# A decode block on one core: whole key rows for three pairs, and diagonal sums moved behind the next pair's scores

## The chip, the core and the metric

The kernel runs on one NeuronCore of a Trainium2 chip. The metric is the device time of one execution in microseconds (us); smaller is better. Its engines appear in the profile as PE (TensorE: matrix products, with PEld for its weight loads), DVE (VectorE), ACT (ScalarE), POOL (GpSimd) and SP (SyncE, which here issues nearly all DMAs). Each engine runs its own list of instructions in order; semaphores order them against each other. Sixteen DMA engines move data between the device memory and the on-chip memory (SBUF); PE writes its results into PSUM, which has eight banks.

## What is computed

One token goes through an attention block with a cache of 16384 positions, and then through a small mixer with an MLP. What matters here is the attention:

```
q = (layernorm(x) @ wq)                       # 32 heads of 128
scores = einsum(q, k_cache) * 128 ** -0.5     # 8 key heads, each shared by 4 query heads
p = softmax(scores)
o = einsum(p, v_cache)
h = x + o.reshape(1, 1, 4096) @ wo
```

The two caches are [8, 16384, 128] in bf16, 33.5 MB each. With wq, wo and the weights of the MLP the core reads 79 MB in all and computes little with each byte.

## The kernel before, in words

The work of the attention goes in four *pairs* of key heads (`PAIRS = 4`, loop at the end of the kernel function, from `load_values(0)` on). The keys of a pair are 8 MB, laid out over 128 partitions with 64 KB each (`pair_rows`); the values likewise. There is one buffer for the keys of a pair, `kb_all`, seen as two halves `kb[0]` and `kb[1]` of 32 KB per partition, one buffer `vb` for the values, and one buffer `kt` for the transposed keys of half a pair.

For each pair j the order is:

1. `clear` (ACT) sets the two score banks to zero; DVE copies the pair's query into `qn` (L740).
2. For each half y: `transpose_keys` (DVE, L655) transposes blocks of the half from `kb[y]` into `kt`, eight *pieces* in one or more instructions; the list `cuts` says where an instruction begins, so `(0, 4)` are two instructions with four pieces each. `scores` (PE, L666) multiplies piece by piece, four matmuls each. A piece of `kt` may be overwritten when its matmuls have run. When the half is transposed, `load_keys` lets SP issue the same half of the next pair into `kb[y]` (L468).
3. `softmax`: DVE takes the maximum (L680), PE spreads it, DVE forms the bias (L687), ACT takes the exponential (L691), DVE transposes the probabilities into `pt` (L695).
4. `unread(16)`: PE runs 16 matmuls whose result nobody reads, in a small loop, between the spread of the maximum and the sums. The loop's length is fixed; it doesn't test whether `pt` is there.
5. `sums` (PE, and a reciprocal on DVE, L715), then `values` (PE, L706), 64 matmuls that wait for `pt` and, through an empty instruction on POOL, for the values' landing.
6. `gather`: DVE adds four blocks of the product up (L722, L725) into `od`, PE multiplies that by a mask (L728), DVE scales the diagonal blocks into `o_m` (L730). Then `load_values` lets SP issue the next pair's values, as soon as PE has read `vb`.

SP runs its list in order: the keys of pair j + 1 (two halves) and then the values of pair j + 1. DVE's list has `gather(j)` ahead of the transposes of pair j + 1. After the last pair come the product with `wo` (L775, loaded into `kb[0]`), a layer norm, and the MLP with `w3` and `w4` (L800, L828, L514, loaded into `kb[1]`), the last slice of `w4` as the last transfer.

PE's program is a real loop over the pairs (`_tensor`): it waits on one DVE semaphore, whose count must grow by the same amount in each pair. Therefore an instruction of DVE may carry a `worth` over one, and `SEEN` and `ROUND` say by how much POOL raises the values' semaphore. `P.part` names the section of the loop that an instruction belongs to.

The buffers that set the order around the change are `kb_all` (who has read it, before SP may refill it), `vb`, and `kt`.

Of the kernel before, what the change touches and what calls it, by code (L numbers as in the profile page):

```python
# [356 lines left out]
NCH = D // 128  # L357
# [4 lines left out]
WO = ((0, 20), (20, 32))  # L362
VP = 1

SEEN, ROUND = 47, 28
W3 = ((0, 4),)
W4 = ((0, 8), (8, 13), (13, 14))
PAIRS = HKV // 2
RPARTS = 6
QPAD = 4 * 7  # L370
KP = 8 * DH
# [9 lines left out]
def bass_sequential_preLN__gqa_block_cached__mixer_s_mlp__decode_kernel(  # L381
# [13 lines left out]
    with ExitStack() as ctx:  # L395
# [71 lines left out]
        def load(name, dst, src, key, by="SP", also=()):  # L467
            P.op(by, lambda e: e.dma_start(dst, src), w=[key, *also], dma=name)  # L468
# [24 lines left out]
        def dve(fn, r=(), w=(), bank=(), own=None):  # L493
            return P.op("DVE", fn, r, w, bank, own=own)
# [7 lines left out]
        def pe(fn, r=(), w=(), bank=(), also=(), times=None, many=1):  # L502

            return P.op("PE", fn, r, w, bank, also=also, times=times, many=many)

        def unread(times):
            field = qb[:, :, :, :].rearrange("p a j q -> p (a j q)")
            P.op("PE", lambda e: e.matmul(O_ps[1][:, :], field[:, 0:128], field[:, 0:512], start=True, stop=True),  # L508
                 r=["qb"], bank=[("O", 1)], times=times)
# [77 lines left out]
        load("wq0", wq_sb[:, 0:WQ], wq_in[:, 0:WQ], "wq0")  # L587
        load("wq1", wq_sb[:, WQ:NCH * HQ * DH], wq_in[:, WQ:NCH * HQ * DH], ("v", 0), also=[("v", x) for x in range(1, VP)])
        load_keys(0, 0)
        load_keys(0, 1)  # L590

        dve(lambda e: e.memset(mean4[:, :], -1.0 / (32 * D)), w=["mean4"])
        pool(lambda e: e.memset(ident_f[:, :], 0.0), w=["ident_f"])
# [54 lines left out]
                qcol[lo:hi, :, :, 0].rearrange("p n (j h) -> p n j h", h=REP)), r=["qcol"], w=["qb"])  # L648


        def transpose_keys(y, cuts):
            for t, n in zip(cuts, [b - a for a, b in zip(cuts, [*cuts[1:], 8])]):
                view = lambda x, t=t, n=n: x[:, :].bitcast(I32).rearrange("p (x l w) -> p x (l w)", x=2, l=64)[
                    :, :, t * 512:(t + n) * 512]
                P.op("DVE", lambda e, view=view: e.transpose(view(kt), view(kb[y])),  # L655
                     r=[("r", y, i) for i in range(RPARTS)], w=[("kt", t + i) for i in range(n)], worth=n)

        def key_piece(at, n):
            part = kt[:, :].rearrange("p (x f) -> p x f", x=2)[:, :, bass.ds(at, KP)]
# [18 lines left out]
        def softmax(j):  # L678

            dve(lambda e: e.tensor_reduce(mx[:, :], s_all, AX.X, ALU.max), r=[("s", 0), ("s", 1)], w=["mx"], **both)  # L680
# [6 lines left out]
            dve(lambda e: e.scalar_tensor_tensor(nmh[:, :], nm[:, :, :].rearrange("p g h -> p (g h)"),  # L687
                                                 32 * D * SCALE, zd[:, :].rearrange("p (n d) -> p n d", d=4)[:, :, 0],
                                                 ALU.mult, ALU.mult, accum_out=bias[:, :]),
                r=["nm", "zd"], w=["nmh", "bias"])  # L690
            act(lambda e: e.activation(p_sb[:, :], s_all, ACTF.Exp, bias=bias[:, 0:1], scale=float(SCALE),  # L691
                                       accum_out=acc[:, :]),
                r=[("s", 0), ("s", 1), "bias"], w=["p", "acc"], **both)
            for g in range(2):
                dve(lambda e, g=g: e.transpose(pt[64 * g:64 * g + 64, :, :, g, :], p_sb[64 * g:64 * g + 64, :]),  # L695
                    r=["p"], w=["pt"])
# [14 lines left out]
        def sums(j):  # L711

            pe(lambda e: e.matmul(n_ps[0:32, 32:33], zd[:, :], acc[:, :], start=True, stop=True),  # L713
               r=["acc", "zd", "pt"], w=["n"], bank=["mn"])
            dve(lambda e: e.reciprocal(den[:, :], n_ps[0:32, 32:33]), r=["n"], w=["den"], bank=["mn"])  # L715
        def gather(j):

            O, key = O_ps[0], ("O", 0)
            for c in range(4):
                block = O[:, c * 128:(c + 1) * 128]  # L720
                if c == 0:
                    dve(lambda e, block=block: e.tensor_scalar(od[:, :], block, rowc[:, 0:1], None, ALU.mult),  # L722
                        r=[key, "rowc"], w=["od"], bank=[key])
                else:
                    dve(lambda e, block=block, c=c: e.scalar_tensor_tensor(  # L725
                        od[:, :], block, rowc[:, c:c + 1], od[:, :], ALU.mult, ALU.add),
                        r=[key, "rowc", "od"], w=["od"], bank=[key])
            pe(lambda e: e.matmul(A_ps[0:32, 0:128], zo[:, :], od[:, :], start=True, stop=True),  # L728
               r=["od", "zo"], w=["A"], bank=["A"])
            dve(lambda e: e.scalar_tensor_tensor(  # L730
                o_m[32 * j:32 * j + 32, :, :], A_ps[0:32, 0:128].rearrange("p (d r) -> p d r", d=4), den[:, 0:1],
                maskdd[0:32, :].unsqueeze(2).to_broadcast([32, 4, 32]), ALU.mult, ALU.mult),
                r=["A", "den", "maskdd"], w=["o_m"], bank=["A"])
# [24 lines left out]
        for n, (lo, hi) in enumerate(WO):  # L758
# [114 lines left out]
```

## Time and profile before

| | us |
|---|---|
| median of 3 runs | 189.6 (189.52 to 189.7) |
| the profiled execution | 189.84 |
| its span, first to last instruction | 188.5 |
| DVE busy, of that: transposes of keys (L655, 25 instructions) | 116.6, 70.6 |
| PE busy, of that: scores (L666, 256 matmuls) | 131.4, 70.1 |
| mean time of one value matmul / one score matmul | 0.379 / 0.416 |

Times of single instructions come from the profiled execution, counted from the start of its span. In a row of the timeline the first number is the start, the second the duration; then come the engine, the line of the kernel, the operation, the output and its inputs, the shapes, the number of instructions merged into the row, and in brackets how long the engine had been idle and for whom. In a row of the groups, busy time and the mean duration in ns follow the bar, then idle time and what ended it. A row of the DMA view gives the size and the time from issue to landing; "SPq" rows of the timeline give the issue. A row of the stretches gives the stretch, its length, the busy time of PE, PEld, DVE, ACT and POOL with the number of instructions, the granted TensorE clock (1.00 is full), the busy share of the DMA engines and their GB/s.

### The profile page before, as it was taken

Reading aid. Unit: us, or ns where it says so; the run is one execution under the profiler, and the core shown is the slowest. Engines: PE = TensorE matmul, PEld = TensorE weight load, DVE = VectorE, ACT = ScalarE, POOL = GpSimd, SP = SyncE. Lnnn points to the kernel's source line nnn. Section 1 sums busy time; section 2 is a strip of 40 time slices with the busy share of each in tenths; the row PEclk is TensorE's granted clock in tenths of the full one; section 3 lists DMA queues with packets and bytes.
Section 4 is the critical chain, followed back from the end, with each engine's and each line's share of the span. In section 5 each row is a group of like instructions: output and inputs, shape, how many; then the busy total and the mean of one; then the engine's idle time right before and its main releaser. Section 6 shows DMA issues by size and latency. Waiting matters only on the chain.

```text
span 188.5 us, 2406 instructions
## 1 busy us (share of the span) xinstructions
PE 131.4 (70%) x767; PEld 51.1 (27%) x767; DVE 116.6 (62%) x139; ACT 13.7 (7%) x21; POOL 4.6 (2%) x8
## 2 busy tenths in 40 slices
PE   0109902978879419888794198887947999696783
PEld 0103401333324203333242033332422333133321
DVE  5740599699152597891525978915259997543165
ACT  3000100000040000000400000004000000320012
POOL 8100000000000000000000000000000000000000
PEclk9999985599999966999999669999996999999789
DMA  6999999999799999988999999997999999969994
GB/s 227 468 417 445 445 445 445 445 445 445 334 445 445 445 556 417 431 348 382 424 445 445 445 445 445 445 445 341 438 445 445 556 445 431 431 297 404 423 414 162
DMA packets 2895, 79.19 MB, mean 420 GB/s; under 512 B 334, under 2 KB 462, under 8 KB 718
## 3 DMA queue, kind: packets, MB, share of 16 engines
q1 hardware_dynamic: 2886, 79.17, 97.7%
q8 instruction: 1, 0.02, 0.0%
q10 hardware_dynamic: 8, 0.00, 0.0%
HBM read 79.17 MB, written 0.00 MB: 420 GB/s over the span
## 4 chain that ended last, share of the span: by engine, by line
PE 51%; DVE 35%; DMA 6%; issue 6%; ACT 0%; SPq 0%; DVEq 0%; ACTq 0%
DVE kt L655 25%; PE banks L666 20%; PE banks L508 12%; PE banks L706 8%; DMA vb<-in_A_wq_dram 6%; PE banks L632 5%; DVE mx L680 3%; PE banks L775 2%; DVE od L725 2%; PE banks L683 1%; PE banks L728 1%; DVE od L722 1%; DVE qcol L639 1%; DVE mxd L681 1%; PE banks L828 1%
## 5 line engine op out<-in xcount | busy, mean ns | idle before, releaser
L666 PE MATMUL banks<-kt,qn 128*128 x256 | 70.1, 416 | 25.6 <-DVE kt L655 25.4
L655 DVE STREAM_TRANSPOSE kt<-kb 128x4096 int32<-128x4096 int32 (+2 forms) x25 | 70.6, 2878 | 5.2 <-PE banks L666 5.2
L666 PEld LDWEIGHTS banks<-kt,qn 128*128 x256 | 26.2, 102 | 68.9 <-issue 53.5
L508 PE MATMUL banks<-qb 128*128 128x512 bf16 x70 | 25.6, 389 | 0.6
L706 PE MATMUL banks<-vb,pt 128*32 128x512 bf16 x256 | 14.7, 379 | 0.0
L632 PE MATMUL banks<-vb,xn 128*128 x32 | 10.0, 489 | 6.7 <-DVE xn L623 6.7
L691 ACT ACTIVATE p_sb<-banks,bias 128x1024 bf16<-128x1024 f32 x4 | 4.5, 1114 | 132.7 <-DVE nmh L687 132.7
L680 DVE TENSOR_REDUCE mx<-banks 128x1 f32<-128x1024 f32 x4 | 4.9, 1225 | 14.6 <-PE banks L666 14.6
L695 DVE STREAM_TRANSPOSE pt<-p_sb 64x1024 bf16<-64x1024 bf16 x8 | 9.9, 1239 | 5.4 <-ACT p_sb L691 5.3
L508 PEld LDWEIGHTS banks<-qb 128*128 128x128 bf16 x70 | 6.7, 97 | 18.8 <-issue 18.5
L706 PEld LDWEIGHTS banks<-vb,pt 128*32 128x32 bf16 x256 | 9.3, 97 | 3.5
L639 DVE STREAM_TRANSPOSE qcol<-banks 64x1024 f32<-64x1024 f32 x4 | 4.8, 1227 | 8.2 <-PE banks L632 8.2
L722 DVE TENSOR_SCALAR od<-banks,rowc 128x128 f32<-128x128 f32 x4 | 1.4, 350 | 13.4 <-PE banks L706 13.4
L632 PEld LDWEIGHTS banks<-vb,xn 128*128 128x128 bf16 x32 | 3.8, 120 | 12.5 <-issue 10.6
L683 PE MATMUL banks<-mxd,mean 128*128 128x128 f32 x8 | 2.0, 326 | 6.6 <-DVE mxd L681 6.6
L728 PE MATMUL banks<-od,zo 128*32 128x128 f32 x8 | 1.6, 285 | 6.5 <-DVE od L725 6.5
L675 ACT ACTIVATE banks<-mean 128x1024 f32<-128x1024 f32 x4 | 4.1, 1027 | 20.1 <-DVE qcol L639 20.0
L775 PE MATMUL banks<-kb,o_b 128*32 128x512 bf16 x44 | 4.6, 550 | 1.1 <-DVE o_b L771 1.1
L715 DVE RECIPROCAL den<-banks 32x1 f32<-32x1 f32 x4 | 0.6, 155 | 6.9 <-PE banks L713 6.9
L725 DVE SCALAR_TENSOR_TENSOR od<-banks,rowc,od 128x128 f32<-128x128 f32 x12 | 4.2, 351 | 0.4
L601 PE MATMUL banks<-x,quarter 4*128 4x128 bf16 x1 | 0.3, 281 | 5.4 <-DVE quarter L599 5.4
L599 DVE CAST quarter<-ident_f 4x128 bf16<-4x128 f32 x1 | 3.2, 3229 | 1.0 <-DMA x<-in_A_x_dram 1.0
(71 smaller groups left out, 39.9 us busy)
## 6 DMA issues: line engine op xcount, KB each, us to landing
kb<-in_A_k_cache_dram SPq DMA_DIRECT2D x8, 4096.0 KB, 25.5
vb<-in_A_wq_dram SPq DMA_DIRECT2D x1, 3584.0 KB, 11.7
kb<-in_A_wo_dram SPq DMA_DIRECT2D x1, 2560.0 KB, 24.1
kb<-in_B_w_dram SPq DMA_DIRECT2D x1, 1792.0 KB, 23.1
kb<-in_A_wo_dram SPq DMA_DIRECT2D x1, 1536.0 KB, 27.4
kb<-in_B_w_dram SPq DMA_DIRECT2D x1, 1024.0 KB, 25.2
kb<-in_B_w_dram SPq DMA_DIRECT2D x1, 640.0 KB, 26.3
vb<-in_A_wq_dram SPq DMA_DIRECT2D x1, 512.0 KB, 3.7
```

Of the source, the lines that this page charges most:

```text
L508: P.op("PE", lambda e: e.matmul(O_ps[1][:, :], field[:, 0:128], field[:, 0:512], start=True, stop=True), r=["qb"], bank=[("O", 1)], times= ...
L632: pe(lambda e, k=k: e.matmul(row[:, bass.ds(P.b + P.b0, 512)], copies(xn[:, k:k + 1], 128), wq_k[:, k, bass.ds(P.c + P.c0, REP * DH)], sta ...
L639: dve(lambda e, g=g, b=b, half=half: e.transpose(qcol[64 * g:64 * g + 64, 2 * b:2 * b + 2, :, :].rearrange("p e m u -> p (e m u)"), half.r ...
L655: P.op("DVE", lambda e, view=view: e.transpose(view(kt), view(kb[y])), r=[("r", y, i) for i in range(RPARTS)], w=[("kt", t + i) for i in r ...
L666: pe(lambda e, n=n: e.matmul(row[:, bass.ds(P.y, 512)], qn[:, n, bass.ds(P.q, 128)], key_piece(P.k, n), start=False, stop=(n == 3), skip_g ...
L675: act(lambda e: e.activation(s_all, copies(mean4[:, 0:1], 1024), ACTF.Identity, scale=0.0), r=["mean4", "p"], w=[("s", 0), ("s", 1)], **both)
L680: dve(lambda e: e.tensor_reduce(mx[:, :], s_all, AX.X, ALU.max), r=[("s", 0), ("s", 1)], w=["mx"], **both)
L691: act(lambda e: e.activation(p_sb[:, :], s_all, ACTF.Exp, bias=bias[:, 0:1], scale=float(SCALE), accum_out=acc[:, :]), r=[("s", 0), ("s", ...
L695: dve(lambda e, g=g: e.transpose(pt[64 * g:64 * g + 64, :, :, g, :], p_sb[64 * g:64 * g + 64, :]), r=["p"], w=["pt"])
L706: pe(lambda e, l=l, ct=ct, ch=ch: e.matmul(O_ps[0][32 * ct:32 * ct + 32, :], pt[:, l, ch, :, :].rearrange("p g u -> p (g u)"), tiles[:, l ...
L725: dve(lambda e, block=block, c=c: e.scalar_tensor_tensor(od[:, :], block, rowc[:, c:c + 1], od[:, :], ALU.mult, ALU.add), r=[key, "rowc", ...
L775: pe(lambda e, r_=r_, q=q: e.matmul(O_ps[0][32 * q:32 * q + 32, :], copies(o_b[:, r_:r_ + 1], 32), wo_sb[:, r_ * D:(r_ + 1) * D], start=(r ...
```

## The change

The keys of pairs 0 to 2 come as one transfer with whole rows of 64 KB, issued once the second half of the pair before has been read; pair 3 still comes in halves. ACT copies the last two of the eight pieces of the second half into a new buffer `aside`, and DVE transposes these two from there, so its last read of `kb_all` is one instruction earlier. The cuts change: the second half of pairs 0 to 2 takes three instructions with 4, 2 and 2 pieces, pair 3 takes (2, 2, 4) and (4, 2, 1, 1) instead of (1, 1, 2, 2, 2) and eight single ones. `gather` of pair j moves behind the transposes of pair j + 1 on DVE (`rows`, its matmul, behind the scores on PE; `spread`, its last step, behind the bias). For pair 0, where nothing is to be gathered, DVE zeroes `od`. The reciprocal goes along with `gather`. `unread` makes 12 rounds instead of 16. `SEEN` follows the new counts.

```diff
-SEEN, ROUND = 47, 28
+SEEN, ROUND = 53, 28
+WHOLE, ASIDE = PAIRS - 1, 2
+LAST = ((0, 2, 4), (0, 4, 6, 7))
...
+        aside = sb("aside", [128, 2, ASIDE * KP], BF16)
...
         def load_keys(j, y):
             n = 128 * DH
+            if j < WHOLE:
+                load("k0", kb_all[:, :], pair_rows(A_k_cache, j), ("r", 0, 0),
+                     also=[("r", 0, i) for i in range(1, RPARTS)] + [("r", 1, i) for i in range(RPARTS)])
+                return
             load(f"k{y}", kb[y][:, :], pair_rows(A_k_cache, j)[:, y * n:(y + 1) * n], ("r", y, 0),
...
         load_keys(0, 0)
-        load_keys(0, 1)
...
+        def put_aside():
+            act(lambda e: e.copy(aside[:, :, :], pieces(kb[1], 8 - ASIDE, ASIDE)),
+                r=[("r", 1, i) for i in range(RPARTS)], w=["aside"])
+
+        def transpose_keys(y, cuts, from_aside=False):
             for t, n in zip(cuts, [b - a for a, b in zip(cuts, [*cuts[1:], 8])]):
+                last = from_aside and t == 8 - ASIDE
+                of = aside[:, :, :] if last else pieces(kb[y], t, n)
+                P.op("DVE", lambda e, of=of, t=t, n=n: e.transpose(pieces(kt, t, n).bitcast(I32), of.bitcast(I32)),
+                     r=["aside"] if last else [("r", y, i) for i in range(RPARTS)],
+                     w=[("kt", t + i) for i in range(n)], worth=n)
...
+            spread(j - 1)
...
+        def gather(j):
+            P.part("late", j)
+            if j < 0:
+                P.op("DVE", lambda e: e.memset(od[:, :], 0.0), w=["od"], worth=1 + NCH)
+                return
             dve(lambda e: e.reciprocal(den[:, :], n_ps[0:32, 32:33]), r=["n"], w=["den"], bank=["mn"])
...
+        def rows(j):
             pe(lambda e: e.matmul(A_ps[0:32, 0:128], zo[:, :], od[:, :], start=True, stop=True),
                r=["od", "zo"], w=["A"], bank=["A"])
...
+            if j < WHOLE:
+                put_aside()
             for y in range(2):
                 P.part("half", j, y)
-                transpose_keys(y, (0, 4) if j < PAIRS - 1 else range(8) if y else (0, 1, 2, 4, 6))
+                if j < WHOLE:
+                    transpose_keys(y, (0, 4, 8 - ASIDE) if y else (0, 4), from_aside=y == 1)
+                else:
+                    transpose_keys(y, LAST[y])
                 scores(j, y)
-                if j < PAIRS - 1:
+                if j < PAIRS - 1 and (y or j + 1 >= WHOLE):
                     load_keys(j + 1, y)
+            gather(j - 1)
             P.part("middle", j)
+            rows(j - 1)
             softmax(j)
-            unread(16)
+            unread(12)
             sums(j)
             values(j)
-            P.part("rest", j)
-            gather(j)
             if j < PAIRS - 1:
                 load_values(j + 1)
+        P.part()
+        gather(PAIRS - 1)
+        P.part()
+        rows(PAIRS - 1)
+        spread(PAIRS - 1)
```

More of the change, by code (lines that the diff above doesn't have):

```diff
@@ L648, in bass_sequential_preLN__gqa_block_cached__mixer_s_mlp__decode_kernel, with pieces @@
                 qcol[lo:hi, :, :, 0].rearrange("p n (j h) -> p n j h", h=REP)), r=["qcol"], w=["qb"])
-        def transpose_keys(y, cuts):
-            for t, n in zip(cuts, [b - a for a, b in zip(cuts, [*cuts[1:], 8])]):
[L653 to L656, printed above, removed]
+        def pieces(x, t, n):
+            return x[:, :].rearrange("p (x l) -> p x l", x=2)[:, :, t * KP:(t + n) * KP]
+        def put_aside():
+            act(lambda e: e.copy(aside[:, :, :], pieces(kb[1], 8 - ASIDE, ASIDE)),
+                r=[("r", 1, i) for i in range(RPARTS)], w=["aside"])
+        def transpose_keys(y, cuts, from_aside=False):
+            for t, n in zip(cuts, [b - a for a, b in zip(cuts, [*cuts[1:], 8])]):
+                last = from_aside and t == 8 - ASIDE
[3 more added lines that the diff above has]
+                     w=[("kt", t + i) for i in range(n)], worth=n)
         def key_piece(at, n):
@@ L686, in softmax @@
                                           AX.X, ALU.min), r=["m"], w=["nm"], bank=["mn"])
-            dve(lambda e: e.scalar_tensor_tensor(nmh[:, :], nm[:, :, :].rearrange("p g h -> p (g h)"),
+            P.op("DVE", lambda e: e.scalar_tensor_tensor(nmh[:, :], nm[:, :, :].rearrange("p g h -> p (g h)"),
                                                  32 * D * SCALE, zd[:, :].rearrange("p (n d) -> p n d", d=4)[:, :, 0],
                                                  ALU.mult, ALU.mult, accum_out=bias[:, :]),
-                r=["nm", "zd"], w=["nmh", "bias"])
+                r=["nm", "zd"], w=["nmh", "bias"], worth=1 + (j == 0))
+            spread(j - 1)
             act(lambda e: e.activation(p_sb[:, :], s_all, ACTF.Exp, bias=bias[:, 0:1], scale=float(SCALE),
@@ L714, in sums @@
                r=["acc", "zd", "pt"], w=["n"], bank=["mn"])
-            dve(lambda e: e.reciprocal(den[:, :], n_ps[0:32, 32:33]), r=["n"], w=["den"], bank=["mn"])
         def gather(j):
             O, key = O_ps[0], ("O", 0)
+            P.part("late", j)
+            if j < 0:
+                P.op("DVE", lambda e: e.memset(od[:, :], 0.0), w=["od"], worth=1 + NCH)
+                return
+            dve(lambda e: e.reciprocal(den[:, :], n_ps[0:32, 32:33]), r=["n"], w=["den"], bank=["mn"])
             for c in range(4):
@@ L727, in gather, with spread @@
                         r=[key, "rowc", "od"], w=["od"], bank=[key])
+        def rows(j):
             pe(lambda e: e.matmul(A_ps[0:32, 0:128], zo[:, :], od[:, :], start=True, stop=True),
                r=["od", "zo"], w=["A"], bank=["A"])
+        def spread(j):
+            if j < 0:
+                P.count["DVE"] += 1
+                return
             dve(lambda e: e.scalar_tensor_tensor(
```

## The prediction

> **What bounds the kernel now.** I read the page first: busy shares, the DMA row of the slices, the queues, the chain of the end.
>
> ```profile
> span 188.5 us, 2406 instructions
> PE 131.4 (70%) x767; PEld 51.1 (27%) x767; DVE 116.6 (62%) x139; ACT 13.7 (7%) x21; POOL 4.6 (2%) x8
> DMA  6999999999799999988999999997999999969994
> q1 hardware_dynamic: 2886, 79.17, 97.7%
> PE 51%; DVE 35%; DMA 6%; issue 6%; ACT 0%; SPq 0%; DVEq 0%; ACTq 0%
> ```
>
> The chain names PE and DVE for 86% of the span, and DVE's transposes and PE's scores do alternate in it. But the queue row says that the 16 DMA engines were busy 97.7% of the span. A chain shows only who came last at each step; a resource that never rests can hide behind it. So next I asked the stretches view for everything between the first bytes and the last ones, and the DMA view and SP's timeline, transfer by transfer (issue time in the one, us from issue to landing in the other).
>
> ```profile
> 2.00:186.00 184.00, 130.41 (x715) 50.36 (x718) 115.74 (x137) 12.76 (x20) 3.32 (x2) 0.92 1.00 430
> ```
> ```profile
> 2.12 0.43 SPq L468 DMA_DIRECT2D kb<-in_A_k_cache_dram  x1
> 23.90 0.33 SPq L468 DMA_DIRECT2D vb<-in_A_v_cache_dram  x1
> 46.97 0.33 SPq L468 DMA_DIRECT2D kb<-in_A_k_cache_dram  x1
> 122.47 0.33 SPq L468 DMA_DIRECT2D kb<-in_A_k_cache_dram  x1
> 138.42 0.33 SPq L468 DMA_DIRECT2D vb<-in_A_v_cache_dram  x1
> 160.34 0.43 SPq L468 DMA_DIRECT2D kb<-in_B_w_dram  x1
> ```
> ```profile
> kb<-in_A_k_cache_dram SPq DMA_DIRECT2D x1, 4096.0 KB, 30.2
> vb<-in_A_v_cache_dram SPq DMA_DIRECT2D x1, 27.8
> kb<-in_A_k_cache_dram SPq DMA_DIRECT2D x1, 4096.0 KB, 24.1
> kb<-in_A_k_cache_dram SPq DMA_DIRECT2D x1, 4096.0 KB, 26.2
> vb<-in_A_v_cache_dram SPq DMA_DIRECT2D x1, 29.6
> kb<-in_B_w_dram SPq DMA_DIRECT2D x1, 128.0 KB, 26.1
> ```
>
> From 2 to 186 us the DMA share is 1.00 at 430 GB/s: the stream has no hole. Adding the rows pairwise gives landings: keys 0 (second half) 32.3 us, values 0 51.7, keys 1 71.1, keys 3 148.7, values 3 168.0, the last slice of w4 186.4. Eight MB of keys in rows of 32 KB took 71.1 − 51.7 = 19.4 us, of values in rows of 64 KB 168.0 − 148.7 = 19.3: a difference of the size of the view's 0.1 us. From keys 1 to keys 3, two pairs, it was 77.6 us, so 19.4 for each 8 MB; that puts values 1 at 90.5, keys 2 at 109.9. Now the end, against that last landing:
>
> ```profile
> 185.98 0.99 PE L828 MATMUL banks<-kb,hcol 128*32 128x128 bf16 x52 [1.54 <-DVE hcol L816]
> 186.80 0.23 PE L514 MATMUL banks<-kb,hcol 128*32 128x128 bf16 x4
> ```
>
> The four matmuls that use the last slice start at 186.80, only 0.4 us after it landed. So the kernel has **two chains that end together**: the stream, and PE/DVE 0.4 us behind it. Whatever the edit gives PE and DVE, about 0.4 us of it can reach the end, plus what the stream itself gains.
>
> **The change, part by part.** *Keys of pairs 0 to 2 as one transfer.* The same bytes; three issues fewer on SP (each about 0.3 us there, beside a full queue: nothing). The gain by longer rows lies between 0 and 0.1 us per pair, by the 19.4 and the 19.3; I take 0.2 us for three, and keep 0 to 0.3. The price is lateness: the first half of keys can no longer be used while the second is on its way. Both halves now land at 32.3, 71.0, 109.7 us. At 71.0 the transposes start 5.5 us later than now, as they began at 65.53:
>
> ```profile
> 27.39 8.77 DVE L655 STREAM_TRANSPOSE kt<-kb 128x4096 int32<-128x4096 int32 x2
> 38.12 8.77 DVE L655 STREAM_TRANSPOSE kt<-kb 128x4096 int32<-128x4096 int32 x2 [1.97 <-PE banks L666]
> 65.53 8.75 DVE L655 STREAM_TRANSPOSE kt<-kb 128x4096 int32<-128x4096 int32 x2
> 75.97 8.77 DVE L655 STREAM_TRANSPOSE kt<-kb 128x4096 int32<-128x4096 int32 x2 [1.69 <-PE banks L666]
> 89.05 1.23 DVE L680 TENSOR_REDUCE mx<-banks 128x1 f32<-128x1024 f32 x1 [4.31 <-PE banks L666]
> 160.61 1.22 DVE L680 TENSOR_REDUCE mx<-banks 128x1 f32<-128x1024 f32 x1 [1.67 <-PE banks L666]
> 164.58 2.49 DVE L695 STREAM_TRANSPOSE pt<-p_sb 64x1024 bf16<-64x1024 bf16 x2 [1.33 <-ACT p_sb L691]
> ```
> ```profile
> L655 DVE STREAM_TRANSPOSE kt<-kb 128x4096 int32<-128x4096 int32 x12 | 52.6, 4420 | 5.2 <-PE banks L666 5.2
> L655 DVE STREAM_TRANSPOSE kt<-kb 128x2048 int32<-128x2048 int32 x3 | 6.7, 2271 | 0.0
> ```
>
> *Does the stream stay full?* With one buffer for keys and one for values, keys j+1 must be issued while values j are still arriving. They are issued when the third transpose of the second half has read the buffer (the last two pieces are read from `aside`). Counted from the first transpose: third big one 75.97 − 65.53 = 10.4 us, plus half a pair of them 4.4, plus a two-piece one 2.3: 17.1 us (pair 0: 10.7 + 4.4 + 2.3 = 17.4). Values j land 19.4 us after keys j. So the issue comes 2.0 us (pair 0) and 2.3 us (pairs 1, 2) ahead of the end of the queue. Now values 0 are issued at 23.90, 8.4 us before keys 0 have landed; then only these 2 us are left. The nearest price of an issue into an empty queue is the first transfer of the kernel:
>
> ```profile
> 0.73 0.40 SPq L468 DMA_DIRECT2D vb<-in_A_wq_dram  x1
> vb<-in_A_wq_dram SPq DMA_DIRECT2D x1, 512.0 KB, 3.7
> ```
> ```profile
> DMA packets 18, 0.04 MB, mean 105 GB/s; under 512 B 8, under 2 KB 8, under 8 KB 18
> ```
>
> The second fence is the DMA view of 1.6 to 2.0 us: its packets of 4 KB are the first rows of this transfer, so data flow at most 1.3 us after the issue at 0.73. From above: it landed after 3.7 us, of which 0.5 MB at 430 GB/s are 1.2, so at most 2.5 us are not data. I take 1.3, the direct sighting; then the stream stays full with 0.7 us to spare. Cost 0, with up to 2.5 kept for the range. The Trainium skill, "DMA: Bandwidth & Descriptors", section "Anatomy of one DMA", speaks against the change here: it puts the fixed cost of one DMA at about 2.0 us. It adds that most of this is the receipt of the write, behind the data; if all 2.0 stood ahead of the data, pair 0 would be at its limit, an estimate of 0.0 to 0.1 us lost. No run shows yet which part stands ahead.
>
> *The copy to `aside`* is 4096 elements on ACT; by the clear of 1024 elements it is an estimate of 4 × 1.03 = 4.1 us.
>
> ```profile
> L675 ACT ACTIVATE banks<-mean x4: 1027/1027/1027, 22.8 to 130.7; 128x1024 f32<-128x1024 f32 x4
> ```
>
> ACT has nothing else between clear and exponential, and the reader comes 15 us later: nothing. ACT's wait on the keys holds up only that exponential. Without that cover the fourth transpose would wait, and PE with it.
>
> *Diagonal sums behind the next scores.* These rows are its price:
>
> ```profile
> L725 DVE SCALAR_TENSOR_TENSOR od<-banks,rowc,od 128x128 f32<-128x128 f32 x12 | 4.2, 351 | 0.4
> L728 PE MATMUL banks<-od,zo 128*32 128x128 f32 x8 | 1.6, 285 | 6.5 <-DVE od L725 6.5
> L730 DVE SCALAR_TENSOR_TENSOR o_m<-banks,den,maskdd 32x128 f32<-32x128 f32 x4 | 1.4, 341 | 2.0 <-PE banks L728 2.0
> ```
>
> Four operations on O (4 × 0.35 = 1.4 us) and a reciprocal leave the stretch between values and transposes; they now fill DVE's wait for the scores (4.31 us in the row at 89.05), `rows` (two passes, 0.4 us on PE) lies beside the 1.2 us maximum, `spread` (0.3) inside the 1.33 us wait for the exponential: nothing while these waits last, some 2.2 us per pair if they went. In pairs 0 to 2 the stretch won buys no time: DVE, ready at 32.4 + 23.8 + 6.5 = 62.7 us (steps below), stands before keys that land at 71.0. PE's `unread` loop, 12 in place of 16, ends 1.5 us sooner; there too it waits for values or keys. POOL's one signal per pair stays. Only pair 3, whose keys come in halves, and the tail turn PE/DVE work into time.
>
> *Pair 3, step by step.* Keys 2 land at 109.7, transposes start 109.8. To the maximum it took 89.05 − 65.53 = 23.5 us (0.3 more in pair 0, whose third transpose came 10.7 us in); the split last transpose spares PE 0.2: 133.1. From maximum to the end of the probabilities' transposes it took 164.58 + 2.49 − 160.61 = 6.5: 139.6. The copy of the query, 0.2, then the first half's transposes (8.8): 139.8 to 148.6. Now they begin at 141.0:
>
> ```profile
> 140.99 17.96 DVE L655 STREAM_TRANSPOSE kt<-kb 128x1024 int32<-128x1024 int32 x13
> 152.42 8.16 PE L666 MATMUL banks<-kt,qn 128*128 x32 [0.24 <-DVE kt L655]
> 162.54 6.00 PE L508 MATMUL banks<-qb 128*128 128x512 bf16 x16
> 168.53 0.19 PE L713 MATMUL banks<-acc,zd 128*32 128x1 f32 x1
> ```
>
> The second half lands at 148.7 − 0.2 = 148.5, so it follows at 148.6: a first transpose of four pieces 4.4, the hand-over 0.2, then 8.16 of scores: 161.4, **0.8 us later** than the 160.61 of now, because a big first piece makes PE wait. But behind it PE no longer idles through 16 `unread`: now 162.54 + 6.00 = 168.53, though DVE was done at 164.58 + 2.49 = 167.07. New: 161.4 + 6.5 = 167.9, the sums and then the values at 168.0 to 168.1, 0.4 to 0.5 us earlier. Values 3 land at 168.0 − 0.2 = 167.8, just before.
>
> *The sum.* The compute chain reaches the tail 0.45 us earlier. The last slice lands at 186.2; the last matmuls can start no earlier, so at most 186.80 − 186.25 = 0.55 can be won. Forecast 0.4 to 0.45 us: 189.84 → 189.4 against the profiled run's own time (189.84, span 188.5 and 1.3 around it). The median of the three runs, 189.6, lies 0.2 below that run; there I expect **189.2 us**. A difference under 0.2% (0.38 us) is about what a measurement here cannot tell from none; the forecast stands right at that edge.
>
> A rule that would give more: the same page, "Where 436 GB/s comes from", gives a port ceiling of 435.2 GB/s. The 430 of the row agree to 1%; if long rows lifted the 25 MB of keys to the ceiling, an estimate of 0.7 us would be spared and the sum would be 188.7. The values' 64 KB rows, at 19.4 us, show no such thing.
>
> **The rivals.** *(a) The end does not move.* The unprofiled runs may have their PE/DVE chain already at the last landing, the longer rows may be worth nothing, or the 0.8 us later scores may cost more than the shorter `unread` spares: 0 to 0.25 us won, 189.35 to 189.6. For it: every gain above is smaller than a us. *(b) Slower: a hole in the stream.* Keys j+1 issued too late, behind the third transpose. It decides when the lead needed exceeds 2.0 us; at the 2.5 from above it loses 0.5 + 0.2 + 0.2 = 0.9 us, and a PE at half clock one us longer (its share is 0.92 on the mean) as much again in a pair. 189.6 − 0.4 + 0.9 to 1.9 = 190.1 to 191.1; 190.2 by the first. Against it: the sighting at 1.3. *(c) Pair 3 late:* if the transposes there wait for pair 2, its scores slip by a us more, 0.6 us behind now: 190.1. *(d) It does what it says:* transposes at once after each softmax. A period is (140.99 − 65.53) / 2 = 37.7 us, so 65.53 + 37.7 − (89.05 + 6.5) = 7.7 us per pair, 3 × 7.7 = 23: 167. The stream forbids it: 79.17 MB at 430 GB/s are 184.1 us.
>
> **How the numbers follow.** Forecast (0.25 to 0.55 won) 0.54, of which 0.41 lie beyond 0.2% and 0.13 within; (a) 0.22, within; (b) 0.16 slower; (c) 0.06 slower; (d) and the faster rate 0.02. Faster 0.43, same 0.35, slower 0.22. The range runs from 189.0 (all 0.55 won) to 190.3, which takes in (a), (c) and the lower half of (b); about 0.12 is left out. The forecast's own range is 189.0 to 189.4.
>
> **What would show it.** DMA share 1.00 through 51.7, 90.5 and 129 us, and values 3 landing 0.2 us earlier: stream right; a dip there with a later landing: (b). DVE idle before the first key transposes of pairs 1 and 2 with a DMA as releaser, 8 us each. Maximum of pair 3 near 161.4, values near 168.1. The last four matmuls under 0.2 us behind the last landing. I am wrong if the last landing moves by more than 0.4 us either way.

## The result, and the profile after

The changed kernel takes **190.47 us** (median of 10 runs, 190.15 to 191.38) against 189.62 us before (10 runs, 189.5 to 189.84). The ratio is 1.005, 95% interval 1.0036 to 1.0063: half a per cent slower. The ten runs scatter over 1.2 us where the ten of before scatter over 0.3; beside the experiments the kernel before scattered over 0.8 to 1.0 us in 20 to 23 runs, so the scatter alone says little. The forecast was 189.2, in a range that ended at 190.3. All ratios, here and below, compare fast runs: a run more than 1.5% above the fastest of its kernel is left out (four in `e7`, one in `e5`).

The page of the changed kernel: span, the DMA row and the GB/s of the 40 slices, the chain of the end by engine and by line, and the group of the key transposes.

```profile
span 189.4 us, 2348 instructions
DMA  6999999999959999999999999997999999899994
GB/s 226 466 415 443 443 443 443 443 443 443 429 249 443 443 429 443 443 443 443 443 443 443 443 443 443 443 443 332 443 429 443 512 401 401 374 428 419 434 414 177
DMA 54%; DVE 23%; PE 18%; issue 3%; SPq 1%; ACT 1%; DVEq 0%; ACTq 0%
DMA kb<-in_A_k_cache_dram 39%; DVE kt L668 20%; PE banks L680 18%; DMA kb<-in_B_w_dram 14%; DVE pt L710 1%; SPq L471 1%; DVE mx L694 1%; ACT p_sb L706 1%; PE banks L697 0%; PE banks L865 0%; DVE qn L767 0%; DVE nm L699 0%; DVE mxd L695 0%; DVE fin L872 0%; DVE nmh L701 0%
L668 DVE STREAM_TRANSPOSE kt<-kb 128x4096 int32<-128x4096 int32 (+2 forms) x19 | 63.8, 3407 | 29.4 <-DMA kb<-in_A_k_cache_dram 23.2
```

The chain that named PE and DVE now names the DMA: DVE waits 23.2 us for keys that land whole. The DMA row has one new digit, the 5 in the twelfth slice (52 to 57 us), 249 GB/s there. Such a digit is a hint and no more: the view counts a packet where it starts, and packets of 64 KB start in rounds 2.42 us apart, so that the row of before has a 7 in its eleventh slice although nothing is lost there. The last slice of the GB/s row and the first belong to the two ends, as before. The whole stream:

```profile
2.00:187.00 185.00, 123.41 (x729) 49.73 (x729) 115.74 (x135) 23.57 (x23) 3.32 (x2) 0.87 1.00 428
```

SP's timeline (issues) and the DMA view (us to landing) show which transfer lost time: values 0, keys 1, values 1, keys 2, last slice of `w4`.

```profile
23.53 0.33 SPq L471 DMA_DIRECT2D vb<-in_A_v_cache_dram  x1
50.31 0.33 SPq L471 DMA_DIRECT2D kb<-in_A_k_cache_dram  x1
66.88 0.33 SPq L471 DMA_DIRECT2D vb<-in_A_v_cache_dram  x1
89.03 0.33 SPq L471 DMA_DIRECT2D kb<-in_A_k_cache_dram  x1
160.75 0.45 SPq L471 DMA_DIRECT2D kb<-in_B_w_dram  x1
```
```profile
vb<-in_A_v_cache_dram SPq DMA_DIRECT2D x1, 28.1
kb<-in_A_k_cache_dram SPq DMA_DIRECT2D x1, 21.8
vb<-in_A_v_cache_dram SPq DMA_DIRECT2D x1, 24.5
kb<-in_A_k_cache_dram SPq DMA_DIRECT2D x1, 21.9
kb<-in_B_w_dram SPq DMA_DIRECT2D x1, 128.0 KB, 26.8
```

Values 0 land at 51.6, keys 1 at 72.1: 20.5 us for 8 MB that took 19.4 before. Values 1 land at 91.4 (19.3 later), keys 2 at 111.0 (19.55). The last slice lands at 187.6 instead of 186.5. So 1.1 us were lost at **keys 1**, issued 1.3 us before the landing of values 0, and they stay lost to the end. The span grew by less, some 0.8 us, because the tail behind the last landing is shorter, 189.4 − 187.6 = 1.8 us instead of 2.1.

The packet records of the trace (start and duration of every DMA packet) show where the 1.1 us went. The 16 engines end their last data of values 0 between 50.80 and 51.17 us. Their first packets of keys 1 start between 51.28 and 52.26, so an engine stood idle for 0.55 us on average. And these first packets are slow. The DMA view of 51.25 to 52.30 us has just the 16 of them, the view of 54.15 to 55.20 the 16 behind them:

```profile
q1 hardware_dynamic: 16, 1.05, 288.1%
q1 hardware_dynamic: 16, 1.05, 230.4%
```

The share is of 16 engines over 1.05 us, so a packet took 3.03 us in the first round and 2.42 in the second: 0.6 us more. The lines of DVE that set the issue, and those of pair 3:

```profile
32.38 8.77 DVE L668 STREAM_TRANSPOSE kt<-kb 128x4096 int32<-128x4096 int32 x2 [5.28 <-DMA kb<-in_A_k_cache_dram]
43.61 6.64 DVE L668 STREAM_TRANSPOSE kt<-kb 128x4096 int32<-128x4096 int32 x2 [2.46 <-PE banks L680]
50.18 2.27 DVE L668 STREAM_TRANSPOSE kt<-aside 128x2048 int32<-128x2048 int32 x1
141.75 17.60 DVE L668 STREAM_TRANSPOSE kt<-kb 128x2048 int32<-128x2048 int32 x7
163.31 1.22 DVE L694 TENSOR_REDUCE mx<-banks 128x1 f32<-128x1024 f32 x1 [2.52 <-PE banks L680]
```

Keys 1 are issued when the two instructions of the row at 43.61 are done, at 50.25.

### The profile page after: what moved, and what is told of

It is laid out like the page before. It is cut to its first block, busy times and chain, and to the rows that moved or that the text cites. A ratio compares the mean times of both kernels' runs of the same rounds, so it can differ in the third digit from the quotient of the medians.

```text
span 189.4 us, 2348 instructions
## 1 busy us (share of the span) xinstructions
PE 124.2 (66%) x753; PEld 50.1 (26%) x753; DVE 116.2 (61%) x137; ACT 24.5 (13%) x24; POOL 4.6 (2%) x8
## 4 chain that ended last, share of the span: by engine, by line
DMA 54%; DVE 23%; PE 18%; issue 3%; SPq 1%; ACT 1%; DVEq 0%; ACTq 0%
DMA kb<-in_A_k_cache_dram 39%; DVE kt L668 20%; PE banks L680 18%; DMA kb<-in_B_w_dram 14%; DVE pt L710 1%; SPq L471 1%; DVE mx L694 1%; ACT p_sb L706 1%; PE banks L697 0%; PE banks L865 0%; DVE qn L767 0%; DVE nm L699 0%; DVE mxd L695 0%; DVE fin L872 0%; DVE nmh L701 0%
## 5 line engine op out<-in xcount | busy, mean ns | idle before, releaser
L668 DVE STREAM_TRANSPOSE kt<-kb 128x4096 int32<-128x4096 int32 (+2 forms) x19 | 63.8, 3407 | 29.4 <-DMA kb<-in_A_k_cache_dram 23.2
L515 PE MATMUL banks<-qb 128*128 128x512 bf16 x54 | 19.3, 387 | 0.5
L661 ACT COPY aside<-kb 128x4096 bf16<-128x4096 bf16 x3 | 10.8, 3605 | 30.3 <-DMA kb<-in_A_k_cache_dram 30.3
L515 PEld LDWEIGHTS banks<-qb 128*128 128x128 bf16 x54 | 5.2, 98 | 13.5 <-issue 13.3
L668 DVE STREAM_TRANSPOSE kt<-aside 128x2048 int32<-128x2048 int32 x3 | 6.8, 2269 | 0.0
L812 PE MATMUL banks<-kb,o_b 128*32 128x512 bf16 x44 | 3.9, 526 | 1.1 <-DVE o_b L808 1.1
## 6 DMA issues: line engine op xcount, KB each, us to landing
kb<-in_A_k_cache_dram SPq DMA_DIRECT2D x2, 4096.0 KB, 20.5
```

The costliest lines, as they stand in the source:

```text
L661: act(lambda e: e.copy(aside[:, :, :], pieces(kb[1], 8 - ASIDE, ASIDE)), r=[("r", 1, i) for i in range(RPARTS)], w=["aside"])
L668: P.op("DVE", lambda e, of=of, t=t, n=n: e.transpose(pieces(kt, t, n).bitcast(I32), of.bitcast(I32)), r=["aside"] if last else [("r", y, i ...
```

## The experiments

Three theories stood against each other. **A:** the stream loses time where a transfer is issued too shortly before the queue ends. **B:** the moved sums, the copy or the later scores hold PE and DVE up. **C:** whole rows of keys are themselves slower. "Lead" is the time from an issue to the landing of the transfer ahead of it. "Lost" is what a transfer took from that landing to its own, over the 19.35 us (half a pair of keys: 9.71) of an undisturbed one; landings for this are read from the traces to 0.01 us.

**Pair 0 in halves again** (`e1_first_in_halves`): its transposes start early, so keys 1 get a long lead.

```diff
-            if j < WHOLE:
+            if 0 < j < WHOLE:
                 load("k0", kb_all[:, :], pair_rows(A_k_cache, j), ("r", 0, 0),
...
         load_keys(0, 0)
+        load_keys(0, 1)
```

> The changed kernel, but the keys of pair 0 come in two halves again, so pair 0 is transposed from about 27 us and keys 1 are issued near 45 us, some 7 us before values 0 have landed. Theory A (the stream runs dry at keys 1: the 1.1 us are 2.4 us that a transfer needs from its issue until data flow, less a lead of 1.3 us): keys 1 land near 71.1 us, the last slice of w4 near 186.5, time 189.3 to 189.6. Theory B (the moved diagonal sums, the copy on ACT or the later scores hold PE and DVE up, and these set the end): all of that is still there, so 190.3 or more. Theory C (whole rows of keys are slower in the stream): keys 1 land 20 us or more after values 0, time 190.2 or more.

Measured: 191.64 us, ratio to before 1.0081 (1.0059 to 1.0103). The time is what B and C expect, and A missed it; but keys 1 landed at 71.1, as only A has it. The time went at the next refill. Its rows in SP's timeline and the DMA view (values 1, keys 2), and stretches behind it:

```profile
60.33 0.33 SPq L471 DMA_DIRECT2D vb<-in_A_v_cache_dram  x1
88.17 0.33 SPq L471 DMA_DIRECT2D kb<-in_A_k_cache_dram  x1
```
```profile
vb<-in_A_v_cache_dram SPq DMA_DIRECT2D x1, 30.1
kb<-in_A_k_cache_dram SPq DMA_DIRECT2D x1, 24.2
```
```profile
89.00:91.00 2.00, 2.00 (x9) 0.77 (x8) 1.93 (x4) 0.00 (x0) 0.00 (x0) 1.00 1.00 360
91.00:93.00 2.00, 2.00 (x10) 0.76 (x8) 0.70 (x2) 0.00 (x0) 0.00 (x0) 1.00 1.05 360
```

Values 1 land at 90.4, keys 2 at 112.4: 22.0 us, 2.6 too many, at a lead of 2.3 us. The stretches count 11 packets of 64 KB each (360 GB/s); the shares of 1.00 and 1.05 make 2.9 and 3.05 us of each, not 2.42. By the packet records an engine also stood idle for 0.9 us on average before its first packet of keys 2. So the loss is an empty queue and slow first packets, both. A fixed price of 2.4 us less the lead, as theory A had it, would have been 0.1 us here; it can't be all. What is left of A after this run is that a short lead is dangerous; B and C stay open.

**Only the sums moved** (`e2_halves_sums_moved`): keys in halves for all pairs, no copy.

```diff
-            if j < WHOLE:
+            if False:
                 load("k0", kb_all[:, :], pair_rows(A_k_cache, j), ("r", 0, 0),
...
         load_keys(0, 0)
+        load_keys(0, 1)
...
-            if j < WHOLE:
-                put_aside()
...
-                    transpose_keys(y, (0, 4, 8 - ASIDE) if y else (0, 4), from_aside=y == 1)
+                    transpose_keys(y, (0, 4))
...
-                if j < PAIRS - 1 and (y or j + 1 >= WHOLE):
+                if j < PAIRS - 1:
```

> Only the second part of the change: all keys in halves as before, cuts of pairs 0 to 2 as before, no copy on ACT; the diagonal sums behind the next scores, 12 rounds of unread, the new cuts of pair 3. Theory A: the stream is that of the kernel before (last landing near 186.4 us), the end follows it by 1.8 instead of 2.0 us, so 189.3 to 189.5, a little under before. Theory B: the moved sums hold PE or DVE up, 190 or more. Theory C: as A here, since there are no whole rows of keys.

Measured: 189.62 us beside 189.73 before, ratio 0.9998 (0.9989 to 1.0008). The last slice lands at 186.5 as before, the span is 188.3. The moved sums cost nothing, which refutes B as far as it blames them; the copy and the late scores are not in this run (`e6` has them). The moved sums also gain nothing that can be measured. Its matmuls of the MLP's second product:

```profile
185.37 0.71 PE L864 MATMUL banks<-kb,hcol 128*32 128x128 bf16 x32 [1.74 <-DVE hcol L852]
186.29 0.46 PE L864 MATMUL banks<-kb,hcol 128*32 128x128 bf16 x20 [0.21 <-DMA kb<-in_B_w_dram]
186.58 0.23 PE L521 MATMUL banks<-kb,hcol 128*32 128x128 bf16 x4
```

Its PE arrived at this product 0.6 us sooner than before (185.37 against 185.98), and then the middle slice of `w4` stopped it; the last four start at 186.58 instead of 186.80.

**Small first pieces** (`e3_first_pieces_small`): the third big transpose no longer waits for PE.

```diff
-                    transpose_keys(y, (0, 4, 8 - ASIDE) if y else (0, 4), from_aside=y == 1)
+                    transpose_keys(y, (0, 4, 8 - ASIDE) if y else (0, 1, 2, 4), from_aside=y == 1)
```

> The changed kernel, but the first half of pairs 0 to 2 is transposed in pieces of 1, 1, 2 and 4 instead of 4 and 4, so PE starts 3.3 us sooner and the third big transpose follows the second one without the wait for PE (2.46 us in pair 0, 1.34 in pair 1). Keys 1 and 2 are issued about 2 and 1 us sooner. Theory A: lead 3.5 us at keys 1, the hole is gone, keys 1 land near 71.1 us, time 189.3 to 189.6. Theory B: PE and DVE work is the same in sum and lies elsewhere, time stays within 0.3 us of 190.5. Theory C: unchanged, 190.2 or more.

Measured: 190.16 us, ratio 1.0028 (1.0011 to 1.0044). Leads of 3.8 us at both refills; keys 1 lost 0.5 us, keys 2 0.1. Half way: A's cure is incomplete, and the time is a little under B's and C's.

**No pieces put aside** (`e4_no_aside`): the issue comes 2.2 us later.

```diff
-            if j < WHOLE:
-                put_aside()
...
-                    transpose_keys(y, (0, 4, 8 - ASIDE) if y else (0, 4), from_aside=y == 1)
+                    transpose_keys(y, (0, 4, 6) if y else (0, 4))
```

> The changed kernel without the copy on ACT: the last two pieces are read from the key buffer, so keys 1 and 2 are issued 2.2 us later. Theory A: leads of minus 0.9 us at keys 1 and about 0.2 at keys 2, so holes of 3.3 and 2.2 us instead of 1.1 and 0.1: 4.3 us more than the changed kernel, near 194.8. Theory B: a copy less, time at or under 190.5. Theory C: at most the 2 us by which the issue is later in one pair, under 193.

Measured: 195.24 us, ratio 1.027 (1.0236 to 1.0304). Keys 1 and 2, both issued as the queue ended (leads of −0.2 and 0.0), lost 2.7 and 2.6 us. That is A's direction and sum (5.3 us, expected 5.5), though not its split.

**Both cures** (`e6_aside_four_small_first`):

```diff
-WHOLE, ASIDE = PAIRS - 1, 2
+WHOLE, ASIDE = PAIRS - 1, 4
...
-                    transpose_keys(y, (0, 4, 8 - ASIDE) if y else (0, 4), from_aside=y == 1)
+                    transpose_keys(y, (0, 4) if y else (0, 1, 2, 4), from_aside=y == 1)
```

> The changed kernel with both cures for the late issue: four pieces of the second half are put aside instead of two, and the first half is transposed in pieces of 1, 1, 2 and 4. Keys 1 and 2 are then issued after 8.8 + 4.5 = 13.3 us of transposes, about 6 us before the values in flight have landed. Theory A, widened by the first runs (a transfer that reaches a queue about to run dry starts slowly and unevenly, at a cost of 0.1 to 2.6 us for leads up to about 4 us; leads of 4.4 us and more have cost nothing): no loss, keys 1 at 71.0 us, last landing near 186.4, time 189.3 to 189.6, and a narrow scatter. Theory C (whole rows of keys are themselves slower): 190 or more, as in the changed kernel.

Measured: 189.56 us beside 189.71, ratio 0.9987 (0.9974 to 1.0). Values 0 and keys 1:

```profile
23.68 0.33 SPq L471 DMA_DIRECT2D vb<-in_A_v_cache_dram  x1
45.45 0.33 SPq L471 DMA_DIRECT2D kb<-in_A_k_cache_dram  x1
```
```profile
vb<-in_A_v_cache_dram SPq DMA_DIRECT2D x1, 27.8
kb<-in_A_k_cache_dram SPq DMA_DIRECT2D x1, 25.4
```

Lead 51.5 − 45.45 = 6.0 us, keys 1 at 70.9, 19.4 after values 0: nothing lost. Values 1, keys 2 and values 2 lost 0.3, 0.3 and 0.1 us at leads of 6.2 to 6.9, and the last slice lands at 186.8; there the packet records show no slow start but packets a few per cent longer well into the transfer, for which no run shows a cause. C is refuted, for the whole rows are all there, and so is the rest of B, for a copy of four pieces and the late scores are there too. The same kernel again (`e11_best_again`):

> The version with four pieces put aside and small first pieces once more, to narrow its interval. Theory A: 0.1 to 0.4 us under the kernel before, which is what the two ends allow: the stream up to 0.2 us shorter, the tail up to 0.3. Theory C: 190 or more.

Measured: 189.53 beside 189.69, ratio 0.9992 (0.9982 to 1.0002). This is the best version found, about 0.15 us under the kernel before, at the edge of what can be told.

**Two transfers at the same late time** (`e7_two_transfers_same_time`): rows of 32 KB, lateness as in the changed kernel.

```diff
-                load("k0", kb_all[:, :], pair_rows(A_k_cache, j), ("r", 0, 0),
-                     also=[("r", 0, i) for i in range(1, RPARTS)] + [("r", 1, i) for i in range(RPARTS)])
+                for h in range(2):
+                    P.op("SP", lambda e, h=h: e.dma_start(kb[h][:, :], pair_rows(A_k_cache, j)[:, h * n:(h + 1) * n]),
+                         r=[("kt", 5)], w=[("r", h, i) for i in range(RPARTS)], dma=f"k{h}")
...
-                     r=["aside"] if last else [("r", y, i) for i in range(RPARTS)],
+                     r=["aside"] if last else [("r", y, i) for i in range(RPARTS)] +
+                     [("r", 1, 0)] * (y == 0 and cuts[-1] == 4 and len(cuts) == 2),
```

> The changed kernel, but the keys of pairs 0 to 2 come as two transfers with rows of 32 KB, issued one right behind the other at the moment at which the changed kernel issues its one, and the first transposes wait for both. Theory A (the lateness costs, not the row): the first of the two reaches an almost empty queue and loses 1 us or more over the two pairs, 190.0 to 191.5. Theory C (the whole row or the one large transfer costs): 189.4 to 189.8.

Measured: 190.63 us, the median of five runs (190.04 to 190.85), ratio 1.0048 (1.0033 to 1.0064); four more took 193.4 to 195.3, and no trace shows where those lost more. Values 1 and the two halves of keys 2, then the landings of values 1 and of the first half:

```profile
65.78 0.33 SPq L471 DMA_DIRECT2D vb<-in_A_v_cache_dram  x1
89.03 0.80 SPq L480 DMA_DIRECT2D kb<-in_A_k_cache_dram  x2
```
```profile
vb<-in_A_v_cache_dram SPq DMA_DIRECT2D x1, 24.6
kb<-in_A_k_cache_dram SPq DMA_DIRECT2D x1, 4096.0 KB, 12.1
```

The first half of keys 2 had a lead of 1.4 us and lost 1.0: it landed 10.7 us after values 1, not 9.7. The whole rows of the changed kernel lost 1.1 at 1.3. The parts agree as well: here an engine stood idle for 0.52 us on average (0.55 there), and the first packet, of 32 KB, took 1.73 us instead of 1.21 (3.03 instead of 2.42 there). Keys 1, with a lead of 2.5, lost nothing. Lateness, not the row, as A says.

**Only the rows** (`e8_rows_only`): the kernel before with whole rows, copy and cuts; the sums stay in place. The fence leaves out the lines for the rows, the copy and the cuts, which are those of the change.

```diff
...
             for y in range(2):
                 P.part("half", j, y)
...
-                if j < PAIRS - 1:
+                if j < PAIRS - 1 and (y or j + 1 >= WHOLE):
                     load_keys(j + 1, y)
             P.part("middle", j)
             softmax(j)
             unread(16)
             sums(j)
             values(j)
             P.part("rest", j)
             gather(j)
```

> Only the first part of the change: whole rows, the copy on ACT, and the new cuts; diagonal sums, reciprocal and 16 rounds of unread stand where they stood before. Theory A: issues of keys 1 and 2 come as late as in the changed kernel, since DVE waits 8 us for keys there and the sums fit into that wait; 190.2 to 191.5. Theory B (the moved sums are what costs): at most 189.7.

Measured: 199.99 us, ratio 1.0527 (1.048 to 1.0575). Both missed it: here the sums matter a lot. DVE's rows of pair 3:

```profile
150.41 17.60 DVE L668 STREAM_TRANSPOSE kt<-kb 128x2048 int32<-128x2048 int32 x7
171.94 1.23 DVE L694 TENSOR_REDUCE mx<-banks 128x1 f32<-128x1024 f32 x1 [3.93 <-PE banks L680]
```

The transposes of pair 3 start at 150.41, 8.7 us later than in the changed kernel (141.75), though its keys land in halves and in time. Pair 2 runs late, for its keys land whole, and without the move everything behind its softmax stands ahead of pair 3. The last slice lands at 190.9, 8.8 us before the end, so here it is PE and DVE that set the time. The moved sums pay for the whole rows there; that expectation considered pairs 0 to 2 alone.

**The changed kernel again** (`e9_changed_again`), no edit:

> The changed kernel once more, for a second look at its two short leads. Theory A: keys 1 and 2 are issued 1 to 2.5 us ahead of the landing of the values, and the time from that landing to theirs is above 19.4 us by 0.1 to 2.6 us each, in no fixed proportion to the lead; the sum of the two excesses, less 0.1, is what the last landing is later than 186.4 us.

Measured: 189.66 us, once. Leads of 2.1 and 2.8 us, losses of 0.3 and 0.0 us, last landing 186.6. With little lost, this execution took no longer than the kernel before. The longer lead comes from the clock. The stretches from the first scores of pair 0 on, one of the changed kernel and two of `e9`:

```profile
37.00:42.80 5.80, 5.80 (x14) 2.08 (x15) 4.16 (x1) 0.00 (x0) 0.00 (x0) 0.50 0.83 362
37.00:41.20 4.20, 4.20 (x10) 1.47 (x11) 4.12 (x1) 0.00 (x0) 0.00 (x0) 0.50 0.80 343
41.20:44.00 2.80, 2.80 (x14) 1.25 (x13) 1.22 (x1) 0.00 (x0) 0.00 (x0) 1.00 1.41 609
```

PE was back at full clock 1.6 us sooner, so DVE got its third transpose, and SP its issue, 0.8 us sooner. This is one run, and all ten of the result took 190.15 or more, so how often the lead comes out longer is not shown.

**Four pieces aside, nothing else** (`e5_aside_four`, `ASIDE` 4 and cuts `(0, 4)` for both halves):

> The changed kernel with four pieces put aside instead of two and nothing else: keys 1 and 2 are issued 2.2 us sooner, so leads between 3.5 and 5 us. Theory A: between the changed kernel and the one with leads of 6 us: 189.4 to 190.2; a lead above 4.4 loses nothing, one below it 0 to 2 us. Theory C (whole rows): as the changed kernel, 190.2 to 191.

Measured: 190.03 us, ratio 1.0011 (0.9997 to 1.0026), inside A's range (nine runs from 189.34 to 190.5; a tenth took 203.09); leads of 4.6 and 4.8 us, losses of 0.4 and 0.0. In this trace values 0 lost 0.5 us as well, at a lead of 9.3: their packets took 2.5 us instead of 2.42 over the first half of the transfer, so a loss of this size need not come from the lead.

**A short lead in the kernel before** (`e10_before_late_values`): the decisive one, since nothing of the change is in it.

```diff
-        def load_values(j):
+        def load_values(j, late=()):
...
+                P.op("SP", lambda e: e.dma_start(vb[:, :], pair_rows(A_v_cache, j)), r=late,
+                     w=[("v", x) for x in range(VP)] + [("landed", x) for x in range(VP)], dma="v")
...
+                if j and not y:
+                    load_values(j, [("mark", "half", j, 0, 0)])
                 scores(j, y)
...
-            if j < PAIRS - 1:
-                load_values(j + 1)
```

> The kernel before, with one edit: the values of pairs 1 to 3 are not issued when their buffer is free but only after the first transpose of the pair. No instruction is added to PE, DVE or ACT, and rows and transfers are those of before. Values 1 are then issued near 70 us instead of 63.1, about 1 us ahead of the landing of keys 1 (71.1); values 2 near 108, some 2 to 3 us ahead; values 3 near 142, some 6 us ahead. They are needed 6 us after they land, so PE and DVE have slack for it. Theory A (any transfer that reaches a nearly empty queue starts badly): values 1 land 0.5 to 2.6 us later than 19.4 us after keys 1, the last landing is later by as much, time 190.2 to 192. Against it (something particular to the keys' refill): 189.5 to 189.8, like before.

Measured: 191.44 us, ratio 1.0106 (1.0071 to 1.014). Second half of keys 1, values 1:

```profile
45.17 0.33 SPq L468 DMA_DIRECT2D kb<-in_A_k_cache_dram  x1
68.18 0.33 SPq L481 DMA_DIRECT2D vb<-in_A_v_cache_dram  x1
```
```profile
kb<-in_A_k_cache_dram SPq DMA_DIRECT2D x1, 4096.0 KB, 26.0
vb<-in_A_v_cache_dram SPq DMA_DIRECT2D x1, 24.0
```

Lead 71.2 − 68.18 = 3.0 us, more than the 1 us expected, for PE and DVE came sooner to this point; values 1 land at 92.2, 21.0 us after keys 1 instead of 19.4: 1.7 us lost, and the time is 1.75 us longer. Values 2, with 5.1, and values 3, with 8.4, lost nothing. So the loss appears in the old kernel, for values, from the issue time alone. By the packet records it is not the whole queue here: 14 of the 16 engines were done with values 1 by 90.1 us, and the last two, which got their first packets 2.8 and 3.4 us after the issue, at 91.3 and 91.9. A landing waits for the last engine.

All refills of keys and values in the traces with a lead under 5 us, beside a price of 2.4 us less the lead:

| kernel, transfer | lead us | lost us | 2.4 less lead |
|---|---|---|---|
| e4 keys 1 | −0.2 | 2.7 | 2.6 |
| e4 keys 2 | 0.0 | 2.6 | 2.4 |
| changed, keys 1 | 1.3 | 1.1 | 1.1 |
| e7 keys 2, first half | 1.4 | 1.0 | 1.0 |
| e8 keys 2 | 1.6 | **2.2** | 0.8 |
| e9 keys 1 | 2.1 | 0.3 | 0.3 |
| e1 keys 2 | 2.3 | **2.6** | 0.1 |
| e8 keys 1 | 2.4 | 0.2 | 0 |
| changed, keys 2 | 2.4 | 0.2 | 0 |
| e7 keys 1, first half | 2.5 | 0.0 | 0 |
| e9 keys 2 | 2.8 | 0.0 | 0 |
| e10 values 1 | 3.0 | **1.7** | 0 |
| e8 values 3 | 3.2 | **1.8** | 0 |
| e3 keys 1 / keys 2 | 3.8 / 3.8 | 0.5 / 0.1 | 0 |
| e8 values 1 | 3.9 | 0.2 | 0 |
| changed, e5, e9, values 3 | 4.4 to 4.7 | 0.0 | 0 |
| e5 keys 1 / keys 2 | 4.6 / 4.8 | 0.4 / 0.0 | 0 |

Leads of 5 us and more lost 0.0 to 0.3 in all traces, and 0.5 once (`e5`, values 0). So A's price holds to 0.2 us or so for most of the short refills, and four of them (bold) lost some 1.5 to 2.5 us on top of it.

## Why the prediction was wrong, step by step

*Two chains that end together, the stream the longer one:* right. The DMA share stayed 1.00, and the end moved with the last landing: that came 1.1 us later, far beyond the 0.4 that the prediction named as the sign of being wrong, and the last four matmuls start right behind it (187.62 after 187.58).

*Keys 1 issued 2.0 us ahead:* 1.3. The third transpose came 43.61 − 32.38 = 11.2 us after the first, not 10.7, since PE ran its first scores at half clock for 5.8 us (row 37.00:42.80 above), where the kernel before had 4.8:

```profile
32.00:36.80 4.80, 4.80 (x12) 1.78 (x13) 4.15 (x1) 0.00 (x0) 0.00 (x0) 0.50 1.01 437
```

The sum also left out two steps of 0.1 us, from the landing to the first transpose and from the last read to the issue.

***"I take 1.3, the direct sighting; then the stream stays full with 0.7 us to spare. Cost 0"* is the step that failed.** I had taken the first packet for the moment from which a transfer is at full rate, and the landing for the moment at which the queue ends. Neither is so. The engines end their data 0.5 to 0.8 us before the landing, so the lead of 1.3 us was only 0.5 to 0.8. The first packets of keys 1 start 1.0 to 1.9 us after the issue, all of them behind the last data of values 0, and then take 0.6 us longer than later ones. The 0.55 us of idle time and these 0.6 make the 1.1 us lost. The answer of the DMA view for 1.6 to 2.0 us, from which I took the 1.3, has the slow packets in another of its lines:

```profile
q1 hardware_dynamic: 10, 0.04, 68.8%
```

Ten packets with 68.8% of 16 engines' 0.4 us are 0.44 us for each 4 KB; from 3 us on the records have 0.16. Losses of up to 2.6 us came with leads as long as 2.3 us, of 1.8 with 3.2, so even my upper bound of 2.5 was too low. What happened is rival (b), with its price (0.9 to 1.9 us; measured 1.1 + 0.2 in the trace) and its half clock of one us more, to which I gave 0.16; by its own sum its lower end is 190.1, not 190.2. The fixed cost of about 2.0 us in the Trainium skill, "DMA: Bandwidth & Descriptors", section "Anatomy of one DMA", pointed the right way in its size. That section gives it for DMAs that GpSimd issues, and these are issued by SP; its split, most of it behind the data, is not what these traces show, with 1.0 us and more ahead of the first packet and 0.3 to 0.5 behind the last. As one constant it doesn't describe these starts either, as e10 lost 1.7 us at a lead of 3.0 and e9 nothing at 2.8.

*0.4 to 0.45 us won at the end:* mis-sized. Without the hole, e2 gained 0.0 ± 0.2 us and e6 with e11 some 0.15 to 0.25. The shorter tail is there (in e2 the last four matmuls start 0.1 us behind the landing, in before 0.3), but the slice of `w4` ahead of the last holds PE as well. The profiled run of before was one of its slowest (189.84 in 189.5 to 189.84), so part of the 0.4 may have been its own lateness; no trace of a faster run shows it.

*Longer rows worth 0.2 us:* right in size. Undisturbed, 8 MB of keys took 19.35 us in whole rows and 9.71 + 9.71 = 19.42 in halves, 0.07 us less per pair. In e6's trace the slower packets in the middle took more than that back, and its last landing was 186.8.

*Pair 3:* right in its order. The maximum forecast at 161.4 came at 161.67 in e2, whose stream has no hole, and at 163.31 in the changed kernel. Of these 1.9 us, 1.3 are the later keys 2 (111.0 for 109.7); the rest is pair 2, whose third transpose came 11.1 us after the first, not 10.4, so that pair 3 began late (141.75, its first half having landed at 140.0). That is a smaller form of rival (c), and it doesn't set the end, which follows the last landing. *Moved sums and copy hidden in pairs 0 to 2:* right. The copy took 3.6 us per pair (estimate 4.1).

What stays open is the size of one loss. At leads of 2 to 4 us it lay anywhere between 0 and 2.6. The records show that in the bad cases some engines get their first packet as late as 2.7 to 3.6 us after the issue; no run here shows why these do.

## What to carry to other kernels

Where the DMA engines are busy all along, look at the lead of each transfer over the end of the queue before anything else; an edit that moves an issue later spends this lead, even if no engine has to wait for its data. In this kernel leads of 5 us and more lost 0.3 us at most, but for one whose packets were 3 to 4% slow over half of the transfer; under 4 us the loss was mostly what is missing to 2.4, and in four of 16 refills it was 1.7 to 2.6 us at leads from 1.6 to 3.2. A whole buffer in place of two halves gains 0.07 us per 8 MB from its longer rows here, and it makes both its use and its refill late.

## What the runs showed of the hardware that I had not expected

A transfer starts slowly even where packets are as large as 64 KB. Issued to engines about to run out of work, it gave them their first packets 1.0 us after the issue at the earliest, and the last of the 16 engines got its own after 1.9 to 3.6 us. The first packets then took longer by about the same time at both sizes: 0.6 us for 64 KB (changed kernel), 0.5 for 32 KB (`e7`). So a DMA share of 1.00 doesn't mean full speed, as slow packets count as busy: 360 GB/s at shares of 1.00 and 1.05 in `e1`. And the end of a queue is not the landing: the last data of each key and value transfer in these traces ended 0.3 to 0.5 us before its landing.
